# Batch 1 of a Fourier mixing kernel put into the quarter-matrix form of the batches after it

## The chip, the cores and the metric

The kernel runs on one core of one Trainium2 chip. The metric is the device time of one execution in microseconds (us), as the median of several runs; less is better. TensorE (PE in the profile, its weight loads PEld) multiplies matrices, VectorE (DVE) and ScalarE (ACT) work on rows of 128 partitions, GpSimd (POOL) does the same for data in SBUF, and SyncE (SP) issues most DMAs.

## The reference

There are two stages, both in 32-bit floating point. The input x has 8 batches of 3008 rows with 256 channels.

```python
X = np.fft.fft(x, axis=1)
X = np.fft.fft(X, axis=2)
attn = X.real                      # (8, 3008, 256) -> (24064, 256)
h = attn @ w_in                    # (256, 2048)
g = np.where(h > 0, h, np.exp(np.minimum(h, 0)) - 1)
out = g @ w_out                    # (2048, 256)
```

## The kernel before

**The main loop.** The real part of a two-dimensional transform is even under a joint reversal of row and channel, so the kernel computes only half of the output rows' frequencies, 1504 for each batch, and gets the mirrored rows from the same products. These 8 x 1504 = 12032 columns pass in 47 tiles of 256 columns. A tile takes 8 steps, each for two blocks of 128 of the 2048 hidden columns; a step is called a slot here, 376 in all. In a slot TensorE runs P (`mm_P`, weights Wc against the ring Rr), Q (`mm_Q`, weights Ws against the ring Ir, added into the same PSUM bank H), and seven more products of 256 columns into four accumulators (eight products in the first 16 slots). Between P and Q, VectorE must read the bank: `even_part` computes E = Rb * wex + H, where Rb holds the extra channel (number 128) and wex the last row of the folded weights. TensorE's Q waits for that. Then VectorE forms the mirrored half (`h_minus`, called h in the schedule), ScalarE does the negative parts and exponentials (b+, b-, x+, x-), VectorE the two results (`g_plus` and `g_minus`, g+ and g-), and GpSimd four sums of 128x256 for the products.

**The transform.** The rings Rr, Ir and Rb hold 2048 columns of transformed rows, and are filled ahead of the main loop. For each batch there are four transforms: cosine or sine (`ri`), and even or odd frequencies (`kodd`). Batches 2 to 7 are done in the *quarter* form: rows are loaded in eight classes (`load_quarter`, `load_odd`, near and far halves; `quarter_row`, a ScalarE copy, mends one row), mirrored rows are added (`mirror_sum`, GpSimd), the two halves are added or subtracted (`half_sum`, VectorE), channels are folded (`channel_fold`, GpSimd; `channel_edge`, ScalarE), pairs of rows are combined or twisted (`quarter_pairs`, `shift_pairs`), and then class `Quarter` multiplies by the matrices QM: two halves of four matmuls each, 94 to 188 columns wide. Its results are unfolded by VectorE and written into the rings (`plus`, `minus`). Batches 0 and 1 are done in the older form: class `Dft` multiplies by the matrices MC, two halves of three matmuls each, up to 378 columns wide. For batch 1 the rows come through `load_x` into the four tiles xl, `mirror_folds` makes the folds (tiles eo) with 30 GpSimd operations, and `at_half` places the halves.

**The extra channel.** `load_ext` gathers one channel of all batches as single elements, `fold_ext` and `dft_ext` transform it into one H bank, `ext_side` copies the bank's four parts into SBUF (parts 0 and 1 at slot 30, parts 2 and 3 at slot 33), and `ext_unfold`, `ext_up`, `ext_down`, `ext_rows` finish it on VectorE. It goes to DRAM, and `spread_ext` brings it into Rb and the last partition of Ir.

**The weights.** They are converted and folded in eight chunks in the first 16 slots. Row 127 of a folded chunk is needed as columns (wex). For chunks 0 and 1 two matmuls with a one-column operand do it (`turn_last_row`, then a ScalarE copy, `put_last_row`); for chunks 2 to 7 two DMAs through DRAM do (`spread_last_row`).

**What sets the order.** Nearly every call is an event `at(t, fn)`; events are sorted by t, and the order within each engine's queue is the order of issue. T = 4.8 is one slot. The beginning is a list of names by time (FRONT), where b-4 is b- of slot 4 and Wc3 the copy of chunk 3 into Wc; the main loop's operations have fixed offsets in a slot; row work of batches 2 to 7 is placed by slot numbers. The time t is no clock: an engine runs its queue in order and waits where data or a buffer is missing. H banks rotate through three buffers.

Of the kernel before, what the change touches and what calls it, by code (L numbers as in the profile page):

```python
# [9 lines left out]
FP = mybir.dt.float32  # L10
# [8 lines left out]
ND = 256  # L19
# [6 lines left out]
NE = 377  # L26
# [149 lines left out]
def kernel(  # L176
# [381 lines left out]
    def load_quarter_mats(ri, kodd):  # L558
        t = cpool.tile([128, BW], FP, tag=f"MC{ri}{kodd}", name=f"QM{ri}{kodd}")
        QM[ri, kodd] = t  # L560
        n = sum(QW[i % 2] for i in range(2 * ri + kodd))
        nc.sync.dma_start(
            out=t[0:96, 0 : QW[kodd]], in_=QM_dr.ap()[:, n : n + QW[kodd]]
        )
# [166 lines left out]
    def mirror_folds(L):  # L731

        ops = []
        rows = [t.rearrange("p (m d) -> p m d", d=ND) for t in L]
        for j, k in ((3, 2), (0, 1)):
            own, other = rows[j], rows[k][:, ::-1]
            for m in range(6):
                ops.append(
                    lambda own=own, other=other, m=m: gtt(
                        own[:, m, 1:], own[:, m, 1:], other[:, m, :0:-1], ALU.add  # L740
                    )
                )
            ops.append(
                lambda own=own, other=other: gtt(
                    own[:, :, 0:1], own[:, :, 0:1], other[:, :, 0:1], ALU.add
                )
            )
        EO = [None] * 4
        for kodd in range(2):
            z = L[1 + kodd]  # L750
            for n in range(4):
                c = slice(384 * n, 384 * n + 384)
                ops.append(
                    lambda z=z, c=c, kodd=kodd: gtt(
                        z[:, c], L[0][:, c], L[3][:, c],
                        ALU.subtract if kodd else ALU.add,
                    )
                )
            for ri in range(2):
                t = EO[2 * ri + kodd] = spool.tile(  # L760
                    [128, 768], FP, tag=f"{'eo'[ri]}{1 + 2 * kodd}", bufs=1, name="eo"
                )
                for h in range(2):

                    def fold(z=rows[1 + kodd], t=t, ri=ri, h=h):
                        src = z[:, 3 * h : 3 * h + 3]
                        lo, hi = (
                            v.rearrange("p m (d o) -> p m o d", o=2)
                            for v in (src[:, :, 1:129], src[:, :, 255:127:-1])
                        )  # L770
                        o = t[:, 384 * h : 384 * h + 384]
                        o = o.rearrange("p (m o d) -> p m o d", o=2, d=64)
                        if ri:
                            gtt(o, lo, hi, ALU.subtract)
                        else:
                            gtt(o, lo[:, :, ::-1], hi[:, :, ::-1], ALU.add)

                    ops.append(fold)
                if not ri:
                    o = t.rearrange("p (m o d) -> p m o d", o=2, d=64)  # L780
                    state["edge", kodd] = lambda o=o, z=rows[1 + kodd]: act(
                        o[:, :, 0, 63:64], z[:, :, 0:1]
                    )
        return EO, ops

# [12 lines left out]
    def half_sum(kodd, far, h):  # L798

        n = 94 if far else 96  # L800
        a, b, o = (lines(j, far)[0:n] for j in (0, 3, 1 + kodd))
        for m in (2 * h, 2 * h + 1):
            vtt(o[:, 3 - m], a[:, m], b[:, m], ALU.subtract if kodd else ALU.add)
# [34 lines left out]
    def quarter_pairs(b, ri, kodd, m):  # L838
# [4 lines left out]
        if not kodd:  # L843
            if m == 1:
                state["pairs"] = spool.tile(
                    [128, 384], FP, tag="side", bufs=2, name="pairs"
                )
            new = state["pairs"]
            a, z = (
                t[0:94, 128:512].rearrange("p (m d) -> p m d", d=128)  # L850
                for t in (near, far)
            )
            o = new[0:94].rearrange("p (m d) -> p m d", d=128)
            if m == 1:
                gtt(o, a, z[:, ::-1], ALU.add)
            else:
                gtt(z[:, ::-1], a, z[:, ::-1], ALU.subtract)
            for k in (1, 2, 3):
                parts["u", k] = new[0:94, 128 * k - 128 : 128 * k]
                parts["v", k] = slot(8 - k)  # L860
            return
# [371 lines left out]
    def ext_side(g, rows=NB):  # L1233
        kodd, par = EXT[g]
        n = NO if kodd else NE if par else 2 * NH
        t = spool.tile([128, 384], FP, tag="side", bufs=2, name="side")
        act(t[0:rows, 0:n], state["ext"][32 * g : 32 * g + rows, 0:n])
        state["side", par] = t

    def ext_unfold(kodd, tt, rows=NB):  # L1240
        n = NO if kodd else NE
        h = (n + 1) // 2
        even = state["side", 0]
# [4 lines left out]
    def ext_rows(kodd, tt, rows=NB):  # L1248
        n = NO if kodd else NE
        if not kodd or rows < NB:  # L1250
            rx = spool.tile([128, HALF + 1], FP, tag="rx", bufs=1, name="rx")
            state["rx"] = rx[0:rows]
        rx, a, b = state["rx"], state["es"], state["side", 1][0:rows]
        o, base = 1 - kodd, kodd * RUN
        m = n - 2 * o
        tt(rx[:, base : base + n], a[:, 0:n], b[:, 0:n], ALU.add)
        top = base + RUN - 1
        tt(rx[:, top : top - m : -1], a[:, o : o + m], b[:, o : o + m], ALU.subtract)
        if not kodd:
            tt(rx[:, HALF:], a[:, 0:1], b[:, 0:1], ALU.subtract)  # L1260
            nc.sync.dma_start(
                out=r4_dr.rearrange("o b -> b o"), in_=rx[:, HALF : HALF + 1]
            )
        nc.sync.dma_start(
            out=r128_dr[0:rows, base : base + RUN], in_=rx[:, base : base + RUN]
        )

    def ext_up():
        rx = state["rx"] = spool.tile(
            [128, HALF + 1], FP, tag="rx", bufs=1, name="rx"  # L1270
        )[0:NB]
        a, b = state["es"], state["side", 1][0:NB]
        vtt(rx[:, 0:NE], a, b[:, 0:NE], ALU.add)
        vtt(rx[:, HALF:], a[:, 0:1], b[:, 0:1], ALU.subtract)

    def ext_down():
        rx, a, b = state["rx"], state["es"], state["side", 1][0:NB]
        vtt(
            rx[:, RUN - 1 : RUN - 1 - (NE - 2) : -1],
            a[:, 1 : NE - 1], b[:, 1 : NE - 1], ALU.subtract,  # L1280
        )
        nc.sync.dma_start(
            out=r4_dr.rearrange("o b -> b o"), in_=rx[:, HALF : HALF + 1]
        )
        nc.sync.dma_start(out=r128_dr[0:NB, 0:RUN], in_=rx[:, 0:RUN])
# [398 lines left out]
    def open_x(b):  # L1684
        state["L"], state["loads"] = load_x(b)

# [47 lines left out]
    names["L"] = lambda: [open_x(1)] + [state["loads"][n]() for n in (4, 5)]  # L1734
    for n in range(4):
        names[f"L{n}"] = lambda n=n: state["loads"][n]()
    for slot in range(8):
# [37 lines left out]
        (16.44, "w3p u3b Wc2 Xb1 b+3 w3R h3"),  # L1775
        (17.88, "w4b b-3 J-even u1M w4l w3s x-3"),
        (19.2, "P4 x+3 u2l u2b w3M Xa2 u3d V4"),
        (20.51, "w4d g-3 u2d w3P Q4 g+3 J-copy"),
        (21.72, "w4a Xb2 b+4 u2R J-sum w4p h4"),
        (23.12, "x+4 f3 u2a L1 P5 g+4 Ws3"),  # L1780
# [3 lines left out]
        (28.7, "b-5 P6 w4s u3p L2 J-odd x-5"),  # L1784
        (30.87, "V6 w4M Xa4 g+5"),
        (32.25, "u3s L3 Q6 w4P g-5 Xb4 b+6 h6 J-up J-down u3M"),
# [34 lines left out]
    for c, t in ((2, 15.2435), (3, 23.1265)) + tuple((c, (2 * c - 1) * T + 0.04) for c in range(4, 8)):  # L1821
        at(t, lambda c=c: spread_last_row(c))
    for i in range(8):
        at((12.9 + 0.5 * i) * T + 3.6, lambda i=i: sum_weights(i))
# [73 lines left out]
    def at_half(step, d, par, col):  # L1898
        assert step + 1 >= safe(col)
        t = step * T  # L1900

        def run():
            d().ps = bank("H")
            d().mms(par, d().ps)

        at(t + 4.75, run)
        if par:
            at(t + T + 1.01, lambda: d().plus())
            at(t + T + 1.02, lambda: d().minus())
        else:  # L1910
            at(t + T + 0.9, lambda: d().copy())
            at(t + T + 1.0, lambda: d().unfold())

    def at_dft(step, gap, b, ri, kodd, stat):
        box = []

        def d():
            if not box:
                box.append(Dft(ri, b, kodd, stat()))
            return box[0]  # L1920

        at_half(step, d, 0, 0)
        at_half(step + gap, d, 1, b * HALF + (kodd + 1) * RUN)

    def begin_folds():
        L = state["L"]
        state["EO"], state["ops"] = mirror_folds(L)

# [5 lines left out]
    at(11 * T + 3.55, lambda: ext_rows(1, gtt, 1))  # L1934
    at(11 * T + 3.6, lambda: spread_ext(0, 1))
    for n in range(16):
        j, k = divmod(n, 4)
        at(
            (14.4 + 0.5 * n) * T,
# [7 lines left out]
    at(30 * T + 4.25, lambda: ext_unfold(0, vtt))  # L1947
    at(31 * T + 4.25, ext_up)
    at(32 * T + 4.25, ext_down)
# [159 lines left out]
```

## Time and profile before

| | us |
|---|---|
| median of 3 runs | 1909.23 (1909.05 to 1913.21) |
| the profiled execution | 1909.52 |
| its span, first to last instruction | 1907.7 |
| TensorE busy | 1899.9 (100%) |
| VectorE busy | 1466.4 (77%) |
| GpSimd busy | 1348.9 (71%) |
| ScalarE busy | 877.1 (46%) |

The granted TensorE clock is full throughout. In the profile a 32-bit matmul appears as two records. A line of a timeline gives the start in us from the span's beginning, the duration of the stretch, engine, line, operation, what is written from what, shapes, and the number of instructions merged; in brackets stands the idle time before it and what ended it. Line 592 is the helper that issues every matmul, 598, 601 and 604 are those for VectorE, GpSimd and ScalarE. Slot numbers against time in the trace: slot 6 begins at 60.2 us, slot 8 at 73.5, slot 10 at 86.8, slot 12 at 98.1, slot 14 at 110.3, slot 30 at 193.6, slot 33 at 207.95.

### The profile page before, as it was taken

Reading aid. Unit: us, or ns where it says so; the run is one execution under the profiler, and the core shown is the slowest. Engines: PE = TensorE matmul, PEld = TensorE weight load, DVE = VectorE, ACT = ScalarE, POOL = GpSimd, SP = SyncE. Lnnn points to the kernel's source line nnn. Section 1 sums busy time; section 2 is a strip of 40 time slices with the busy share of each in tenths; the row PEclk is TensorE's granted clock in tenths of the full one; section 3 lists DMA queues with packets and bytes.
Section 4 is the critical chain, followed back from the end, with each engine's and each line's share of the span. In section 5 each row is a group of like instructions: output and inputs, shape, how many; then the busy total and the mean of one; then the engine's idle time right before and its main releaser. Section 6 shows DMA issues by size and latency. Waiting matters only on the chain.

```text
span 1907.7 us, 27911 instructions
## 1 busy us (share of the span) xinstructions
PE 1899.9 (100%) x8972; PEld 1649.8 (86%) x8972; DVE 1466.4 (77%) x2788; ACT 877.1 (46%) x1711; POOL 1348.9 (71%) x1834
## 2 busy tenths in 40 slices
PE   9999999999999999999999999999999999999999
PEld 6888888888888888888888888888888888888887
DVE  8766667887878878778777787877878778777666
ACT  5754444444444444444444444444444444444443
POOL 4887667786677766777667777687766777556664
PEclk9999999999999999999999999999999999999999
DMA  8145211211011110111112111022110210100101
GB/s 339 45 33 43 57 24 45 52 24 36 12 44 41 32 33 12 46 40 30 31 19 49 34 28 30 13 56 44 24 24 16 55 20 16 17 12 15 20 12 23
DMA packets 278934, 73.80 MB, mean 39 GB/s; under 512 B 254402, under 2 KB 268998, under 8 KB 278788
## 3 DMA queue, kind: packets, MB, share of 16 engines
q1 hardware_dynamic: 270148, 61.58, 15.9%
q0 software_dynamic: 6464, 10.18, 1.7%
q8 instruction: 71, 1.16, 0.3%
q14 instruction: 75, 0.61, 0.1%
q10 hardware_dynamic: 2176, 0.26, 0.1%
HBM read 47.10 MB, written 24.80 MB: 38 GB/s over the span
## 4 chain that ended last, share of the span: by engine, by line
PE 97%; DVE 2%; DMA 0%; issue 0%; ACT 0%; POOL 0%; ACTq 0%; POOLq 0%; DVEq 0%
PE H L592 38%; PE pB L592 17%; PE pC L592 17%; PE pD L592 17%; PE pA L592 9%; DMA xl<-in_x_dram,ix 0%; DVE e L689 0%; DVE o L689 0%; POOL w L601 0%; DVE E L1339 0%; DVE pow L460 0%; DVE w L418 0%; DVE v L598 0%; DVE u L598 0%; ACT Wsc L604 0%
## 5 line engine op out<-in xcount | busy, mean ns | idle before, releaser
L601 POOL TENSOR_TENSOR G<-G 128x256 f32<-128x256 f32 x1437 | 1045.8, 737 | 504.1 <-DVE G L1369 346.9
L604 ACT ACTIVATE G<-H 128x512 f32<-128x512 f32 x376 | 224.4, 597 | 929.1 <-DVE G L1353 925.5
L1339 DVE SCALAR_TENSOR_TENSOR E<-Rb,wex,H 128x256 f32<-128x256 f32 x752 | 327.6, 477 | 334.3 <-PE H L592 327.6
L592 PE MATMUL H<-Rr,Wsc 128*128 128x256 f32 x1504 | 387.7, 380 | 0.5 <-ACT Wsc L604 0.5
L592 PE MATMUL H<-Ir,Wsc 128*128 128x256 f32 x1504 | 386.8, 380 | 1.0 <-DVE E L1339 1.0
L592 PE MATMUL pC<-G,WT 128*128 128x256 f32 x1440 | 369.6, 379 | 0.0
L592 PEld LDWEIGHTS H<-Ir,Wsc 128*128 128x128 f32 x1504 | 278.4, 189 | 48.9 <-DVE E L1339 3.4
L592 PEld LDWEIGHTS H<-Rr,Wsc 128*128 128x128 f32 x1504 | 282.1, 190 | 41.6 <-issue 2.3
L592 PEld LDWEIGHTS pC<-G,WT 128*128 128x128 f32 x1440 | 273.6, 190 | 37.2
L1353 DVE SCALAR_TENSOR_TENSOR G<-E,H 128x512 f32<-128x512 f32 x376 | 256.9, 683 | 45.1 <-POOL G L601 11.5
L1369 DVE SCALAR_TENSOR_TENSOR G<-G,H 128x512 f32<-128x512 f32 x376 | 255.8, 680 | 39.6 <-ACT G L604 39.5
L1369 DVE SCALAR_TENSOR_TENSOR G<-M,G 128x512 f32<-128x512 f32 x376 | 256.6, 682 | 0.7 <-ACT M L604 0.7
L604 ACT ACTIVATE G<-G 128x512 f32<-128x512 f32 x376 | 233.4, 621 | 0.0
L592 PE MATMUL pA<-G,w 128*128 128x256 f32 x784 | 229.4, 379 | 0.0
L592 PE MATMUL pB<-G,w 128*128 128x256 f32 x784 | 229.4, 379 | 0.0
L592 PE MATMUL pD<-G,w 128*128 128x256 f32 x784 | 229.3, 379 | 0.0
L604 ACT ACTIVATE M<-G 128x512 f32<-128x512 f32 x376 | 224.2, 596 | 2.8 <-DVE G L1353 1.5
L604 ACT ACTIVATE M<-M 128x512 f32<-128x512 f32 x376 | 221.1, 588 | 0.1
L592 PE MATMUL pB<-G,WT 128*128 128x256 f32 x720 | 214.4, 379 | 0.0
L592 PE MATMUL pD<-G,WT 128*128 128x256 f32 x720 | 214.2, 379 | 0.0
L592 PEld LDWEIGHTS pA<-G,w 128*128 128x128 f32 x784 | 148.9, 190 | 20.7 <-DVE G L1369 0.3
L592 PEld LDWEIGHTS pB<-G,w 128*128 128x128 f32 x784 | 148.9, 190 | 20.4 <-PE H L592 0.2
(172 smaller groups left out, 1555.3 us busy)
## 6 DMA issues: line engine op xcount, KB each, us to landing
out_dram<-ot SPq DMA_DIRECT2D x496, 32.0 KB
xq<-in_x_dram SPq DMA_DIRECT2D x48, 94.0 KB
out_dram<-ot SPq DMA_DIRECT2D x256, 2.0 KB
Rb<-r SPq DMA_DIRECT2D x10, 376.0 KB
raw<-in_moe_w_in_dram SPq DMA_DIRECT2D x7, 512.0 KB
MC<-dft_mats SPq DMA_DIRECT2D x3, 943.5 KB
xq<-in_x_dram SPq DMA_DIRECT2D x12, 192.0 KB
xq<-in_x_dram SPq DMA_DIRECT2D x36, 64.0 KB
```

The source lines that it names most:

```text
L592: nc.tensor.matmul(out_, lhsT=lhsT, rhs=rhs, start=start, stop=stop, skip_group_check=True)
L601: pin(nc.gpsimd.tensor_tensor(out=o, in0=a, in1=b, op=op))
L604: pin(nc.scalar.activation(out=o, in_=i, func=func, **kw))
L1339: nc.vector.scalar_tensor_tensor(out=S.E[:, c], in0=Rb[:, cols(i)], scalar=wex[:, f : f + 1], in1=S.H[:, c], op0=ALU.mult, op1=ALU.add,)
L1353: nc.vector.scalar_tensor_tensor(out=two(S.G[:, 0:512])[:, :, ::-1], in0=two(S.E), scalar=2.0, in1=two(S.H), op0=ALU.mult, op1=ALU.subtract,)
L1369: nc.vector.scalar_tensor_tensor(out=o, in0=e, scalar=-1.0, in1=h, op0=ALU.add, op1=ALU.max)
```

## The change

Batch 1 takes the quarter form. `mirror_folds`, `open_x`, `at_half`, `at_dft` and `begin_folds` go; batch 1's loads, sums, folds, pairs and twists become a table of single times, and four calls of `at_quarter` place its transforms. The four QM matrices are packed into the homes of MC[1,0] and MC[1,1] and loaded at slot 7.2 in place of slots 51 to 60; the twist table and the index tables of the quarter loads come early too. For batch 1 the combined pairs go into free columns of the fold tiles in place of a `side` buffer. The extra channel's bank is copied in one go at slot 30: parts 2 and 3 then go into the free part of the tile rx, and its later steps are cut into `ext_up`, `ext_down`, `ext_put` and placed by the table. Its element loads begin 0.8 slot later. For weight chunks 6 and 7 the last row is turned by TensorE.

```diff
-    def load_quarter_mats(ri, kodd):
...
+    def load_quarter_mats():
+        n = 0
+        home = [
+            cpool.tile([128, BW], FP, tag=f"MC1{i}", name=f"QM{i}") for i in range(2)
+        ]
+        for ri in range(2):
+            for kodd in range(2):
+                w = QW[kodd]
+                c = 0 if ri else QW[1 - kodd]
+                QM[ri, kodd] = t = home[ri == kodd][:, c : c + w]
+                nc.sync.dma_start(out=t[0:96], in_=QM_dr.ap()[:, n : n + w])
+                n += w
...
-    def mirror_folds(L):
...
     def ext_side(g, rows=NB):
         kodd, par = EXT[g]
         n = NO if kodd else NE if par else 2 * NH
-        t = spool.tile([128, 384], FP, tag="side", bufs=2, name="side")
+        if kodd and rows == NB:
+            t = state["rx"][:, RUN + NO * (1 - par) :]
+        else:
+            t = spool.tile([128, 384], FP, tag="side", bufs=2, name="side")
...
-    names["L"] = lambda: [open_x(1)] + [state["loads"][n]() for n in (4, 5)]
+    names["L"] = lambda: [
+        fn(1, j, 0) for j in (3, 0) for fn in (load_quarter, load_odd)
+    ]
...
-    for c, t in ((2, 15.2435), (3, 23.1265)) + tuple((c, (2 * c - 1) * T + 0.04) for c in range(4, 8)):
+    for c, t in ((2, 15.2435), (3, 23.1265)) + tuple((c, (2 * c - 1) * T + 0.04) for c in (4, 5)):
         at(t, lambda c=c: spread_last_row(c))
+    for c in (6, 7):
+        at((2 * c - 1) * T + 3.02, lambda c=c: turn_last_row(c))
+        at((2 * c - 1) * T + 3.03, lambda c=c: put_last_row(c))
...
-            (14.4 + 0.5 * n) * T,
+            (15.2 + 0.5 * n) * T,
             lambda j=j, k=k: load_ext(j, 192 * k, 192 * (k + 1)),
...
-    at(33 * T + 1.46, lambda: ext_side(2))
-    at(33 * T + 1.47, lambda: ext_side(3))
...
-    at(27 * T + 4.3, quarter_table)
-    at(34 * T, lambda: nc.sync.dma_start(out=twist_tab[0:96], in_=QT_dr.ap()))
...
-    for step, ri, kodd in ((26, 0, 0), (34, 1, 0), (37, 0, 1), (42, 1, 1)):
-        at_dft(step, 2, 1, ri, kodd, lambda k=2 * ri + kodd: state["EO"][k])
...
+    at(30 * T + 1.48, ext_open)
+    for g in (2, 3):
+        at(30 * T + 1.49, lambda g=g: ext_side(g))
+    at(10.0, quarter_table)
+    at(7.2 * T, load_quarter_mats)
+    at(8 * T, lambda: nc.sync.dma_start(out=twist_tab[0:96], in_=QT_dr.ap()))
...
+    for t, fn, *key in (
+        (22.73, mirror_sum, 3, 0, 3),
+        (25.32, quarter_row, 1),
...
+        (36.22, mirror_sum, 0, 0, 2),
+        (38.68, half_sum, 1, 0, 1, vtt),
+        (39.31, half_sum, 1, 0, 0, vtt),
+        (40.40, channel_fold, 0, 1, 0, 0),
+        (44.12, half_sum, 0, 0, 1, vtt),
...
+        (148.01, ext_unfold, 0, vtt),
+        (153.06, ext_up, 0, vtt),
+        (157.11, ext_down, 0, vtt),
...
+        (279.33, ext_put, 1),
+        (279.72, spread_ext, 1, 1),
+    ):
+        at(t, lambda fn=fn, key=key: fn(*key))
+
+    for step, ri, kodd, finish, join in ((28, 0, 0, 0, 31), (34, 1, 0, 0, 37), (38, 0, 1, 42, 53), (44, 1, 1, 50, 54)):
+        at_quarter(step, 1, ri, kodd, finish, join)
```

## The prediction

> **What bounds the kernel now.** I read the page's first part and its chain first.
>
> ```profile
> span 1907.7 us, 27911 instructions
> PE 1899.9 (100%) x8972; PEld 1649.8 (86%) x8972; DVE 1466.4 (77%) x2788; ACT 877.1 (46%) x1711; POOL 1348.9 (71%) x1834
> ...
> PE 97%; DVE 2%; DMA 0%; issue 0%; ACT 0%; POOL 0%; ACTq 0%; POOLq 0%; DVEq 0%
> ```
>
> TensorE is busy all the time and is 97% of the chain. The end moves only by matmul time removed or added, and by gaps in TensorE's stream. Busy time counts overlapping records, so I price a group of matmuls by its spacing: from its first start to the start of what follows. The timeline of TensorE has one half of a batch 1 transform (three matmuls, two records each), and one of batch 2:
>
> ```profile
> 173.20 1.44 PE L592 MATMUL H<-MC,eo 128*128 128x189 f32 x6
> 174.48 1.02 PE L592 MATMUL H<-Rr,Wsc 128*128 128x256 f32 x4
> ...
> 431.88 0.36 PE L592 MATMUL H<-QM,e 95*128 95x95 f32 x2
> 432.07 0.39 PE L592 MATMUL H<-QM,o 94*128 94x95 f32 x2
> 432.30 0.39 PE L592 MATMUL H<-QM,pairs 94*128 94x95 f32 x2
> 432.52 0.39 PE L592 MATMUL H<-QM,o 94*128 94x94 f32 x2
> 432.74 1.06 PE L592 MATMUL H<-Rr,Wsc 128*128 128x256 f32 x4
> ```
>
> 174.48 - 173.20 = 1.28 us against 432.74 - 431.88 = 0.86 us. Then the gaps: lines of TensorE's timeline with a wait in brackets, and of VectorE's.
>
> ```profile
> 60.21 1.13 PE L592 MATMUL H<-Rr,Wsc 128*128 128x256 f32 x4 [0.54 <-ACT Wsc L604]
> ...
> 101.58 1.13 PE L592 MATMUL H<-Ir,Wsc 128*128 128x256 f32 x4 [0.69 <-DVE E L1339]
> ...
> 215.49 1.13 PE L592 MATMUL H<-Ir,Wsc 128*128 128x256 f32 x4 [0.31 <-DVE E L1339]
> ```
>
> ```profile
> 99.45 0.43 DVE L406 TENSOR_SCALAR pow<-raw 128x512 int32<-128x512 int32 x1 [2.15 <-POOL w L601]
> ...
> 112.11 0.87 DVE L1339 SCALAR_TENSOR_TENSOR E<-Rb,wex,H 128x256 f32<-128x256 f32 x2 [1.43 <-DMA wex<-wx]
> ```
>
> A 256-column matmul starts every 0.432 us. What the spacing shows beyond that, the restart included, is 0.8 us before 60.2 (slot 6), 0.96 us before 101.6 (slot 12), 0.23 us at 112.7 (slot 14) and 0.7 us before 215.5 (slot 34). From 216 to 1497 no gap passes 0.1 us, although five batches with quarter matrices lie there. These four, 2.7 us, are all that scheduling can win in the stretch that the change touches.
>
> **What the Trainium skill says.** (1) TensorE: Matmul & The Clock Gate, section LDWEIGHTS: a load takes columns/1.2 ns, 107 for 128 columns, whatever the rows. The trace agrees on rows (192 ns for 94x128, 190 for 128x128; these records overlap). Eight records at 107 ns would be 0.86 us, an estimate that matches the spacing: narrow quarter matmuls are bound by weight loads, so fewer columns save less than in proportion. (2) SBUF — State Buffer, section SBUF: two separate sides: a VectorE operation with two SBUF inputs and a GpSimd operation that reads SBUF exclude each other for a whole instruction. The trace agrees: the same VectorE adds of 256 columns take 482 to 949 ns. (3) DMA: Bandwidth & Descriptors, section Anatomy of one DMA: about 2.0 us fixed, given for GpSimd's path. Here SyncE's wex copy, issued at 109.96, releases VectorE at 112.11: 2.15 us.
>
> **Part 1, matmuls of batch 1.** Out go 24 with MC, in eight groups of 1.28, 1.90, 1.28, 1.91, 1.26, 1.90, 1.27 and 1.90: 12.70 us. In come 32 with QM, as in every later batch: 0.86, 1.09, 0.87, 1.08, 0.87, 0.87, 0.87, 0.86: 7.37 us. All of it lies on the path: **-5.33 us**, the surest term.
>
> **Part 2, last weight row of chunks 6 and 7.** Two DMAs each go (wx, then wex); two 128x1 matmuls and a ScalarE copy (0.17 us, hidden, ScalarE is 46% busy) each come. The same pair starts at 35.24 and the next matmul at 35.71, 0.47 us: **+0.94** for both. The wait at 112.11 goes: **-0.23**. The H bank of folds[6] and folds[7] is kept half a slot longer and is wanted two slots later: 0.
>
> **Part 3, extra channel.** Before, sides 2 and 3 (0.98 us of ScalarE at 209.84) and the p copy stood ahead of an exponential at 210.73; VectorE idled 1.48 us for it, E came late, TensorE lost 0.7 us. They move to slot 30; slot 33 has the p copy alone, as later tiles, which don't stall there: **-0.7** (0 if the twists put there refill it). At slot 30 four copies of 0.47 us end near 195.7: g+ starts 0.65 us late, and the VectorE work up to the E of 199.5 still fits: 0 (at worst +0.5). The bank freed earlier makes room for the quarter transforms. The put of the second half moves to slot 58.2; slot 64 needs it: 0.
>
> **Part 4, row work of batch 1.** *GpSimd*: out 22 xl operations (12 at 0.94, 8 at 1.00, 2 at 0.30 us) and 8 eo at 1.18, 29 us; in 16 mirror sums at 0.72, 4 edges at 0.2, 16 folds at 0.84 and the pairs, about 4.6 together: 30 us. The total stays. *VectorE*: 16 half-sum adds, 20 twists and the quarter's unfolds come, long unfolds and puts go; by mean spacings +5 us in slots 7 to 10, +5 in 20 to 28, +14 in 28 to 46, +4 to 58. In slots 28 to 46 that is 81 us of work in about 99, 82%; between 431 and 520, where batch 2 does the same, VectorE was busy 69.30 of 89.00 us and TensorE had no gap. The cover is VectorE's wait for H before each E; where it is gone, a late E costs TensorE its lateness. I take **+0.4** (0 to 2). *SyncE and DMA*: 4 row loads and the 4 copies of part 2 go, 32 row loads come; net 24 at about 0.4 us, 10 us of SyncE's queue, mostly before slot 15, while the DMA engines are 2 to 52% busy. The element loads of the extra channel queue behind them, and are set 0.8 slot later. GpSimd reads their result at 187.4 and TensorE at 191.6, cover 3.2 us after GpSimd's 1 us: 0. Four QM loads (0.36 us each) move from 214 to 277 back to before slot 16; they wait for the last use of MC[1,0] and MC[1,1], near 63 us, and batch 1 wants them at slot 29: 0. Twist table and iotas (0.5 us of SyncE and GpSimd, idle early): 0.
>
> **Part 5, the front.** Slot 6: ScalarE's row copy (0.39 us, spacing 0.30) now stands between b-4 and x-4 in the chain x-4, g-4, h5, b+5, Wc3 that TensorE awaits: **+0.3** (0 to 0.4). Slot 8: two half-sum adds stand ahead of E, which followed at 74.85 without any idle and may start at 75.2 at the latest (Q at 76.09 less 0.87). Two adds at 0.41 us free or 0.72 contended (the operation before them was, 1.51 us) make it 0.45 to 1.1 late, with restart up to 1.2, and slot 9's E is then near its limit: **+1.1** (0 to 2). The next four adds fall into the 2.89 us that VectorE idled before 87.98: 0. Slot 12: E stood behind a VectorE step that waited for GpSimd's multiply at 98.14, which waited for ScalarE (96.69); less GpSimd work doesn't shorten this. But the first pair of part 2 lies between slots 11 and 12 and uses up half of that gap: **-0.47** (-0.96 to 0).
>
> **Sum**: -5.33 + 0.94 - 0.23 - 0.7 + 0.4 + 0.3 + 1.1 - 0.47 = -4.0 us. The profiled execution took 1909.52 us (1907.7 between first and last instruction), 0.3 above the median 1909.23; applied to the median this gives **1905.2 us**. With every open term at its better end: -5.33 + 0.94 - 0.23 - 0.7 - 0.96 = -6.3, 1902.9; all at the worse: -5.33 + 0.94 - 0.23 + 0.5 + 2 + 0.4 + 2 = +0.3, 1909.5. A measurement of this kernel tells some 0.3%, 5.7 us, from no change, so the likeliest gain lies inside that.
>
> **Rivals.** *A, the gaps close* (0.33): slot 8 has room, slots 12, 14 and 34 close: 1902.9 to 1903.5. For it: three of four gaps lose a cause. Against: VectorE had no idle before slot 8. *B, the gaps only move* (within the forecast): -4.4 plus as much new gap as old goes, 1904.8, up to 1909. *C, slower* (0.10): VectorE becomes the bound in slots 33 to 46, where each E stands behind twists and puts. If each is as late as at 215.5, 0.7 us, 14 slots cost 9.8, and -4.0 + 9.8 = +5.8: 1915. From 0.7 us of mean lateness in all 14 it decides. Against: the same work leaves no gap in batches 2 to 7. *D, it does not do what it says*: the order of the built instructions has 24 MC matmuls fewer, 32 QM and 4 one-column matmuls more, so 0.
>
> **How the numbers follow.** Forecast with B 0.57 (within 0.3%), A 0.33 (faster), C with milder relatives 0.10 (slower). The range 1902.8 to 1908.3 takes the better end and most of the worse; all bad terms together, and C, stay out.
>
> **What would show it.** Right: no MC,eo rows; QM groups of 0.86 to 1.09 us between slots 28 and 48; 0.47 us for a pick pair; no wait for wex near 112 and no gap near 215; VectorE about 28 us busier, GpSimd equal; a new gap at slot 8. Wrong: a row of waits for E in slots 31 to 50, or TensorE waiting for the extra channel.

## The result, and the profile after

The change makes the kernel slower: 1921.88 us median of six runs (1919.13 to 1923.29) against 1909.17 for the kernel before (six runs, 1909.05 to 1913.21). The ratio is 1.0063, 95% interval 1.0053 to 1.0073. The forecast was 1905.2 with a range up to 1908.3, so the sign is wrong. The profiled execution took 1920.93 us.

First the page's first and fourth part, of the changed kernel:

```profile
span 1919.1 us, 28089 instructions
PE 1899.6 (99%) x8996; PEld 1651.3 (86%) x8996; DVE 1497.3 (78%) x2854; ACT 878.7 (46%) x1717; POOL 1355.9 (71%) x1846
PE 91%; DVE 2%; DMA 2%; SPq 2%; issue 1%; POOL 1%; ACT 0%; ACTq 0%; DVEq 0%; POOLq 0%
```

TensorE's busy time is the same within 0.3 us, and its share of the chain fell from 97% to 91%: the lost time is waiting, and DMA and SyncE's queue (SPq) are now in the chain. TensorE's waits, in total, times, longest:

```profile
PE H L598 <- DVE E L1285: 6.3, 4, 2.3
PE H L598 <- POOL xe L607: 6.3, 1, 6.3
PE H L598 <- ACT Wsc L610: 1.3, 2, 0.7
```

These five waits for E and xe are in TensorE's timeline (start, stretch, line, idle time before it and its end in brackets), beside two rows that the prediction asked for, a pair of `turn_last_row` and a half of a batch 1 transform:

```profile
52.71 1.13 PE L598 MATMUL H<-Ir,Wsc 128*128 128x256 f32 x4 [2.26 <-DVE E L1285]
...
81.94 1.13 PE L598 MATMUL H<-Ir,Wsc 128*128 128x256 f32 x4 [1.93 <-DVE E L1285]
...
97.24 1.13 PE L598 MATMUL H<-Ir,Wsc 128*128 128x256 f32 x4 [1.62 <-DVE E L1285]
...
104.25 0.50 PE L598 MATMUL H<-pick,Wsc 128*128 128x1 f32 x4
...
109.68 1.13 PE L598 MATMUL H<-Ir,Wsc 128*128 128x256 f32 x4 [0.50 <-DVE E L1285]
...
191.81 0.36 PE L598 MATMUL H<-QM,e 95*128 95x95 f32 x2
...
192.68 1.06 PE L598 MATMUL H<-Rr,Wsc 128*128 128x256 f32 x4
...
203.88 3.92 PE L598 MATMUL H<-MC,xe 128*8 128x189 f32 x24 [6.26 <-POOL xe L607]
207.73 1.13 PE L598 MATMUL H<-Rr,Wsc 128*128 128x256 f32 x4
```

What released VectorE's E in slots 4 and 10, and what it did before slot 8's E; and what GpSimd waited for at slot 30:

```profile
51.78 0.87 DVE L1285 SCALAR_TENSOR_TENSOR E<-Rb,wex,H 128x256 f32<-128x256 f32 x2 [2.27 <-DMA wex<-wx]
...
77.18 2.19 DVE L418 TENSOR_SCALAR w<-raw 128x512 int32<-128x512 int32 x1
79.29 1.81 DVE L604 TENSOR_TENSOR xq<-xq,xq 96x256 f32<-96x256 f32 x2
81.03 0.86 DVE L1285 SCALAR_TENSOR_TENSOR E<-Rb,wex,H 128x256 f32<-128x256 f32 x2
...
96.32 0.87 DVE L1285 SCALAR_TENSOR_TENSOR E<-Rb,wex,H 128x256 f32<-128x256 f32 x2 [2.47 <-DMA wex<-wx]
...
107.54 0.43 DVE L406 TENSOR_SCALAR pow<-raw 128x512 int32<-128x512 int32 x1 [2.08 <-POOL w L607]
```

```profile
203.08 0.39 POOL L607 TENSOR_TENSOR xs<-xs 128x96 f32<-128x96 f32 x1 [9.19 <-DMA xq<-in_x_dram]
```

That line names a row load (xq) as the releaser. It can't be: the operation reads xs. The releaser is inferred from semaphores, and SyncE's queue shows which DMA it was, the last copy into xs, issued at 200.56. Here is that queue before (first fence) and after (second), cut to the extra channel's loads and what stands ahead of them. L1169 and L1126 are the element loads, L1197 and L1154 the copies into xs:

```profile
110.39 6.37 SPq L1169 DMA_DIRECT2D x<-in_x_dram  x4
...
180.42 0.58 SPq L1197 DMA_DIRECT2D xs<-xe_dr  x1
```

```profile
114.41 0.24 SPq L1231 DMA_DIRECT2D r<-rx  x1
119.00 0.65 SPq L334 DMA_DIRECT2D xq<-in_x_dram  x1
119.69 0.96 SPq L317 DMA_DIRECT2D xq<-in_x_dram  x2
...
127.17 0.63 SPq L334 DMA_DIRECT2D xq<-in_x_dram  x1
127.84 3.16 SPq L317 DMA_DIRECT2D xq<-in_x_dram  x7
131.47 6.33 SPq L1126 DMA_DIRECT2D x<-in_x_dram  x4
...
200.56 0.58 SPq L1154 DMA_DIRECT2D xs<-xe_dr  x1
```

The chain of element loads starts 21.1 us later and ends 20.1 us later. It takes the same 70 us in both kernels: 71 DMAs before and 74 after go through SyncE's queue between its first and last issue, 40 of them output stores. Last, the clock, from the windows view of the changed kernel (length; busy us of PE, PEld, DVE, ACT, POOL; granted clock; DMA share; GB/s):

```profile
50.00:53.80 3.80, 1.54 (x8) 1.03 (x7) 2.02 (x5) 1.31 (x4) 3.72 (x5) 1.00 0.13 46
53.80:57.00 3.20, 3.20 (x10) 2.49 (x9) 3.20 (x7) 1.84 (x3) 1.50 (x2) 0.50 0.96 251
...
203.60:207.70 4.10, 3.82 (x24) 1.52 (x24) 0.00 (x0) 0.00 (x0) 3.29 (x6) 0.54 0.20 52
```

After the wait of slot 4, and in the extra channel's matmuls, TensorE runs at half clock (0.50 in the column behind the engines) for over 3 us. A wait of 2.3 us costs 4 us.

**Where the time went.** The starts of slots (first matmul of P) give a table by stretch that doesn't depend on when the first weights arrive. From run to run that arrival moves the start of slot 0 (the first slot) between 26.2 and 28.5 us, so single runs are compared below by these stretches and not by their totals. All runs of this study, one trace each, in us (x130 to b_xlate were executed once, the last four 6 or 21 times):

| kernel | slots 3-5 | 5-9 | 9-11 | 11-15 | 15-29 | 29-61 | 0-61 |
|---|---|---|---|---|---|---|---|
| before | 12.49 | 25.21 | 13.41 | 22.78 | 71.01 | 164.41 | 324.32 |
| after | 16.71 | 27.55 | 15.30 | 23.24 | 68.64 | 169.82 | 336.25 |
| x130 | 16.69 | 27.56 | 15.17 | 23.35 | 68.64 | 176.38 | 342.78 |
| x144 | 16.68 | 27.55 | 15.05 | 23.48 | 68.63 | 173.08 | 339.46 |
| pinrows | 17.03 | 27.55 | 13.41 | 23.68 | 68.63 | 173.11 | 338.43 |
| hs8 | 18.37 | 26.49 | 16.75 | 23.68 | 68.64 | 170.74 | 339.65 |
| late2 | 16.75 | 27.53 | 14.46 | 24.06 | 68.64 | 163.51 | 329.93 |
| x118d | 17.13 | 27.55 | 14.69 | 23.86 | 92.71 | 161.64 | 352.57 |
| pick25 | 13.45 | 29.61 | 13.86 | 23.34 | 68.64 | 168.53 | 332.43 |
| b_xlate | 12.49 | 25.22 | 13.41 | 22.77 | 71.03 | 174.27 | 334.20 |
| latepick | 13.45 | 27.97 | 13.86 | 23.34 | 68.63 | 162.78 | 325.04 |
| best | 13.46 | 26.18 | 15.69 | 24.89 | 68.64 | 162.78 | 326.63 |
| best2 | 13.45 | 26.23 | 15.51 | 24.19 | 68.63 | 163.00 | 326.00 |
| dmapin | 14.00 | 32.44 | 13.41 | 23.81 | 68.64 | 162.97 | 330.26 |

(Slots 0 to 2 take 15.0 in all of them; each column runs from the start of its first slot to the start of its last.) The change costs +4.22 at slot 4, +2.34 mostly at slot 8, +1.89 at slot 10, +0.46 in slots 11 to 15 and +3.04 from slot 15 to 61, in all +11.93. From slot 61 on the two traces differ by less than 0.1 us.

### The profile page after: what moved, and what is told of

It is laid out like the page before. It is cut to its first block, busy times and chain, and to the rows that moved or that the text cites. A ratio compares the mean times of both kernels' runs of the same rounds, so it can differ in the third digit from the quotient of the medians.

```text
span 1919.1 us, 28089 instructions
## 1 busy us (share of the span) xinstructions
PE 1899.6 (99%) x8996; PEld 1651.3 (86%) x8996; DVE 1497.3 (78%) x2854; ACT 878.7 (46%) x1717; POOL 1355.9 (71%) x1846
## 4 chain that ended last, share of the span: by engine, by line
PE 91%; DVE 2%; DMA 2%; SPq 2%; issue 1%; POOL 1%; ACT 0%; ACTq 0%; DVEq 0%; POOLq 0%
PE H L598 35%; PE pB L598 16%; PE pC L598 16%; PE pD L598 16%; PE pA L598 8%; SPq L1520 1%; DMA x<-in_x_dram 1%; SPq L1126 0%; DMA xl<-in_x_dram,ix 0%; DVE E L1285 0%; POOL w L607 0%; DMA wex<-wx 0%; DMA xq<-in_x_dram,ix 0%; DVE e L695 0%; DMA xq<-in_x_dram 0%
```

## The experiments

**Does the extra channel's chain stand behind the row loads?** Two runs moved its element loads forward.

```diff
-            (15.2 + 0.5 * n) * T,
+            (13.0 + 0.5 * n) * T,        # x130;  (14.4 + 0.5 * n) * T in x144
```

x130: 

> One size changed: the extra channel's sixteen element loads are set from slot 13.0 on instead of 15.2, which puts the first of them ahead of the second set of far row loads in SyncE's queue. Theory T1 (head of line: the element loads stand behind row loads that wait until 127.2 us for their tile): the first element load leaves near 118 to 121 us instead of 131.5, the last copy into xs near 188 instead of 200.1, the 6.3 us wait of TensorE for xe before slot 30 goes with the half clock behind it, -8.3 us: about 1912.6. Theory T3 (the added row loads take the DMA engines' throughput): the element loads take correspondingly longer, the wait stays, 1920 to 1921.

x144: 

> One size changed back: the element loads of the extra channel are set from slot 14.4 on, as in the kernel before, instead of 15.2. Theory T2 (the shift by 0.8 slot, about 5 us, makes the chain late): the last copy into xs moves from 200.1 to about 195, and of the 6.3 us wait of TensorE some 1.3 us stay: about 1914 to 1916. Theory T1 (head of line): only one of the four first element loads gets ahead of the far row loads, the other three stay behind them and their wait until 127.2 us, so the wait stays at 5 us or more: 1919.5 to 1921.

Measured: both got worse. TensorE's wait for xe grew to 12.44 us (x130) and 9.45 us (x144), and slots 29 to 61 took 6.6 and 3.3 us more than in the changed kernel. The single times were 1928.71 and 1926.06. The first element load left at 128.8 and 130.3, or 3.5 and 4.3 us after the start of slot 15 (7.4 in the changed kernel): it was still behind the row load that leaves near 128. The other element loads did not come out earlier, because six far row loads now stood among them: 80 DMAs instead of 74 between first and last issue, 79.6 and 76.0 us instead of 69.7. So undoing the shift by 0.8 slot doesn't remove the wait, and a place further forward in the order doesn't by itself bring the end forward. My T1 expected -8.3 and was wrong in that form; no theory had expected either run to get slower.

**Move the producers ahead of nearly everything, or move the consumer.** In late2 the fold, the matmuls, the copies and the three VectorE steps stand two slots later; in x118d all sixteen element loads stand ahead of most far row loads.

```diff
-    at(29 * T + 1.35, fold_ext)
+    at(31 * T + 1.35, fold_ext)      # late2; dft_ext, ext_side, ext_open likewise
...
-        (148.01, ext_unfold, 0, vtt),
+        (157.61, ext_unfold, 0, vtt),
```

```diff
-            (15.2 + 0.5 * n) * T,
+            (11.78 + 0.25 * n) * T,      # x118d
```

late2: 

> Consumer moved, producers left: the fold of the extra channel on GpSimd, its matmuls, the four bank copies and the three VectorE steps behind them stand two slots (about 10.4 us) later; the element loads stay where they are. Theory T1, in the form that the first four runs leave (SyncE's queue hands out some 74 DMAs in about 70 us from the first element load on, whatever stands first; the load chain is late because it starts 21 us later, at 131.5 instead of 110.4): the last copy into xs is still issued near 200, lands near 203, GpSimd is done by 204.1 and TensorE asks for it near 207: no wait for xe, no half clock, -8.3 us in the stretch from slot 28 to 34. Rival (the wait belongs to the place, such as GpSimd's or ScalarE's order in slot 30): a wait of several us for xe or for E shows up again in slots 31 to 33.

x118d: 

> Producers moved: all sixteen element loads are set from slot 11.78 on, a quarter of a slot apart, right behind the store of the first channel row, so that they stand ahead of most far row loads and of all output stores. T1 (start of the chain decides): first element load near 121.5 (the row of the ring and one far row load are still ahead of it), last copy into xs issued 70 us later, near 191 to 193, wait of TensorE at slot 30 under 1 us, -7 to -8 us. Rival T3 (throughput of the DMA engines: 6144 four-byte elements for each quarter of the channel keep them busy): the far row loads behind the elements land late, GpSimd's and VectorE's mirror sums of slots 18 to 24 wait for them, and the wait at slot 30 shrinks by less than half.

Measured, late2: the matmuls with xe follow without a wait and at full clock.

```profile
209.98 2.09 PE L598 MATMUL H<-MC,xe 128*8 128x189 f32 x24
...
219.67 0.70 PE L598 MATMUL pB<-G,WT 128*128 128x256 f32 x2 [0.92 <-POOL G L607]
```

Slots 29 to 61 take 6.3 us less than in the changed kernel. The 8.2 us (from where xe was wanted, 197.55, to 207.73, less the 2.02 us that these matmuls take at full clock) are gone; 2 us come back as two waits for GpSimd's sums, of which the second line shows the first. The loads themselves were not touched, so lateness against a fixed consumer is all there is to this wait.

Measured, x118d: 1937.72, 16 us worse than the changed kernel. The first element load left at 123.0 and TensorE didn't wait for xe, but the row loads behind the elements landed late, as T3 had it. GpSimd's timeline of x118d, and TensorE's:

```profile
146.98 0.89 POOL L607 TENSOR_TENSOR xq<-xq,xq 94x255 f32<-94x255 f32 x2 [4.71 <-DMA x<-in_x_dram]
...
168.99 0.72 POOL L607 TENSOR_TENSOR xq<-xq,xq 94x255 f32<-94x255 f32 x1 [18.97 <-DMA xq<-in_x_dram]
```

```profile
150.07 1.22 PE L598 MATMUL pB<-G,WT 128*128 128x256 f32 x2 [3.00 <-POOL G L607]
170.44 1.22 PE L598 MATMUL pD<-G,w 128*128 128x256 f32 x2 [14.88 <-POOL G L607]
```

GpSimd's mirror sums wait for rows, its sums G stand behind them in the same queue, and TensorE waits for those. Issuing slowed as well: an element load took 1.61 us of SyncE's queue on average (1.06 in the changed kernel), a row load 1.82 (0.86). Whether the queue or the DMA engines behind it set that pace isn't separated. In every order tried here either the rows or the elements came late between slots 12 and 30.

**Is the late start enough without the new rows?** One size changed in the kernel before:

```diff
-            (14.4 + 0.5 * n) * T,
+            (16.9 + 0.5 * n) * T,        # b_xlate
```

> The kernel before, with one size changed: the element loads of the extra channel are set from slot 16.9 on instead of 14.4; no other part of the change is in it. The changed kernel's first element load left 12.8 us later against the slots than before (7.4 us after slot 14's start instead of 5.3 us ahead of it). If the late start alone is sufficient for the wait at slot 30: before, the last copy into xs was issued at 180.4 and, with some 2.5 us to landing and 1.2 us on GpSimd, was about 7 us ahead of TensorE's 191.3; a start about 13 us later makes TensorE wait 5 to 7 us there and, with the half clock behind it, about +7 to +9 us: 1916 to 1918. Rival (the added row loads are needed for it, as they lengthen the chain or use the DMA engines): the chain is shorter than 70 us when the loads stand closer together, and the wait stays under 2 us, 1909 to 1911.

(What this text calls slot 14's start is the start of slot 15 in the count used elsewhere.) Measured: 1919.13 us, 10 us slower than the kernel before. The first element load kept its place at 109.8, the second left at 133.5; the last copy into xs was issued at 196.1.

```profile
199.46 3.48 PE L592 MATMUL H<-MC,xe 128*8 128x189 f32 x24 [8.39 <-POOL xe L601]
```

The wait of 8.39 us is a little over the 5 to 7 that were expected. A late start of this chain is sufficient, without a row of batch 1 in the quarter form. From the second load on it still took 63 us.

**Why does wex land late in slots 4 and 10?** In pinrows the single-row loads of batch 1 keep the program's order, so those of slot 9 leave behind chunk 5's wex copy; in pick25 the last rows of chunks 2 and 5 go by TensorE.

```diff
-                nc.sync.dma_start(                 # load_odd
+                pin(nc.sync.dma_start(             # pinrows, for b == 1
```

```diff
-    for c, t in ((2, 15.2435), (3, 23.1265)) + tuple((c, (2 * c - 1) * T + 0.04) for c in (4, 5)):
+    for c, t in ((3, 23.1265), (4, 7 * T + 0.04)):      # pick25
...
-    for c in (6, 7):
+    at(17.95, lambda: turn_last_row(2))
+    at(17.96, lambda: put_last_row(2))
+    for c in (5, 6, 7):
```

pinrows: 

> One thing changed: the single-row loads of batch 1 are held to the order of the program, so that those of slot 9 go out behind chunk 5's wex copy and not between wx and wex; at chunk 2 (slot 4) the row loads stay between the two, which makes slot 4 the control. Theory W1 (the row loads ahead of wex in the queue or in the DMA engines delay its landing): wex of chunk 5 is issued at about 89.5 us, lands within 3.5 us, and the 1.9 us gap of slot 10 goes, -1.9 us: 1919.0; the gap of slot 4 stays with its half clock. Rival W2 (wex lands late for another reason, such as a wait for a queue that the trace does not show, or the GpSimd gathers): wex lands 5 us or more after its issue as before and the gap of slot 10 stays above 1 us: 1920 to 1921. What the delayed row loads then do to SyncE's queue behind them is open, +-1 us.

pick25: 

> One part widened: the last weight row of chunks 2 and 5 is turned by TensorE (two one-column matmuls and a ScalarE copy each), as chunks 6 and 7 are, and no longer by two DMAs; row loads unchanged. If the 2.4 us gap at slot 4 (with its half clock, 4.0 us in all) and the 1.9 us gap at slot 10 come from the late landing of wex, both go and 0.94 us is added for two pairs: -5.0 us. Rival (E of slot 4 or 10 is held by VectorE or by H as well): over 1 us of either gap stays.

SyncE's queue in slot 9, in the changed kernel and then in pinrows:

```profile
88.56 0.22 SPq L647 DMA_DIRECT2D wx<-Wsc  x1
88.90 1.27 SPq L334 DMA_DIRECT2D xq<-in_x_dram  x2
90.71 0.39 SPq L650 DMA_DIRECT2D wex<-wx  x1
```

```profile
89.25 0.22 SPq L652 DMA_DIRECT2D wx<-Wsc  x1
90.35 0.38 SPq L655 DMA_DIRECT2D wex<-wx  x1
```

With the two 94-row loads between, wex was issued at 90.71 and released VectorE at 96.32, 5.6 us later. Without them slot 10's E (94.62 in pinrows) follows VectorE's work without idling, and slots 9 to 11 take 13.41 us, exactly as before the change. Slot 4, the control, kept its gap. W1 holds for slot 10. Of the 2.47 us that VectorE had idled there, 1.05 lay in the wait for a turn (2.15 us from the issue of wx to that of wex, against 1.10 in pinrows); the rest lay in the landing. The total did not gain (1923.59): the element chain ended later (203.1 against 201.1), TensorE wanted its result 0.8 us earlier and waited 9.05 us for it. In pick25 both gaps went as well: slots 3 to 5 fell by 3.26 and slots 9 to 11 by 1.44. What is left over the kernel before is 0.45 in slots 9 to 11, one pair, and 0.96 in slots 3 to 5, a pair and a new TensorE wait of 0.35 us behind it for ScalarE's copy. The single time is 1919.08, and the table has -3.8 where -5.0 was expected; part of the difference is that after the unchanged 1.93 us wait of slot 8 the clock now fell to half. The view below cuts the time into windows of 3.41 us, first of the changed kernel and then of pick25 ("Missing: the clock" below says why at these places):

```profile
77.69:81.11 3.42, 2.32 (x11) 1.71 (x9) 3.42 (x4) 2.61 (x5) 3.34 (x5) 1.00 0.00 0
81.11:84.52 3.41, 2.58 (x12) 2.30 (x13) 3.41 (x7) 0.00 (x0) 2.15 (x2) 1.00 0.00 0
84.52:87.93 3.41, 3.41 (x18) 3.00 (x17) 3.41 (x8) 2.63 (x5) 1.28 (x1) 1.00 0.02 5
```

```profile
79.12:82.53 3.41, 1.48 (x8) 1.10 (x7) 3.41 (x7) 0.54 (x2) 2.65 (x4) 1.00 0.00 0
82.53:85.94 3.41, 3.41 (x10) 2.69 (x9) 3.41 (x6) 1.28 (x3) 2.11 (x2) 0.50 0.02 5
```

**Slot 8.** Three runs moved the half-sum adds that stand ahead of slot 8's E: hs8 moved one pair behind that E, best one pair there and one behind slot 9's E (with the parts of latepick), best2 put all four on GpSimd and also moved two of the extra channel's copies on ScalarE behind two exponentials.

```diff
-        (38.68, half_sum, 1, 0, 1, vtt),
+        (39.45, half_sum, 1, 0, 1, vtt),     # hs8
```

hs8: 

> One step moved: the first pair of half-sum adds of batch 1 on VectorE is set behind slot 8's E instead of ahead of it. If the two adds ahead of E make the gap of 2.2 us at slot 8, E starts at about 79.3 and the gap goes: -2.2 us, 1918.7. Rival: VectorE is short of time in slot 8 or 9 whatever stands first (mantissa steps of 2.19 us under contention), then the gap moves behind E or into slot 9: 1920 to 1921.

latepick: 

> Two of the tried parts together in the changed kernel: the extra channel's fold and matmuls two slots later, and the last row of chunks 2 and 5 by TensorE as well. By the spacings of the single runs (-6.3 us and -3.8 us, the latter with 1.6 us of half clock after slot 8 in it) about 10 us less than the changed kernel: 1911 to 1913, if the two do not touch. Rival: with the slots earlier by 5 us against SyncE's queue, the element chain is late again at slot 32, and 2 to 4 us come back: 1914 to 1916.

best: 

> As latepick, and the first two pairs of half-sum adds of batch 1 on VectorE taken away from ahead of slot 8's E: one pair stands behind that E, the other behind slot 9's, so that slot 8 and slot 9 have two and six adds. If the 2.1 us gap of slot 8 comes from the pair ahead of E and slot 9 has room for six (VectorE idled 1.6 us before its E and 0.6 us before slot 10's): -2 us and no half clock there (-1.6): 1907.5 to 1909.5, level with the kernel before or slightly faster. Rival (as the first run with the pair moved showed: the gap moves to slots 8 and 9 in full): 1911 to 1913.

best2: 

> As latepick, with two more edits. The four half-sum adds of slot 8 stand on GpSimd again, behind its mantissa multiply of that slot, where GpSimd idled 4.4 us (it waited for ScalarE); and the two copies of the extra channel's second half on ScalarE stand behind the next two exponentials of slot 32 instead of ahead of them. If the pair of adds ahead of slot 8's E made its 2.1 us gap, that gap goes without a new one, since VectorE loses 3 us of work; if the four copies ahead of an exponential make the 1.1 us wait for GpSimd at slot 33, that goes too: -2.1 and -0.8 us against latepick, 1908 to 1909, 1 us faster than the kernel before or level with it. Rival (VectorE and GpSimd are both full between slots 8 and 12, so work moved on either comes back as lateness): 1 to 2 us of new gaps in slots 9 to 12, 1910 to 1911.

Measured. hs8: slot 8's gap shrank to 0.36 us and two new ones, 0.66 and 1.26, came in slot 9; slots 3 to 15 took 2.5 us more than in the changed kernel, 1.7 of it at slot 4, ahead of the step that was moved and so not explained by it; the other 0.8 is 1.06 less in slots 5 to 9 and 1.9 more behind them. best: slots 5 to 9 fell by 1.8 against latepick, slots 9 to 15 rose by 3.4. (In best one fold reads rows of one class before they are summed; its time stands for the placing alone.) best2: -1.7 and +2.5, and its copies gained nothing (slots 29 to 61 took 0.2 more). The rival's account held each time, the work comes back as lateness, though hs8 as a whole was slower than the rival's range. The four adds that follow slot 9's E show why, first in hs8, where GpSimd is idle at that point, then in best2, where it has the moved adds:

```profile
90.06 1.42 DVE L604 TENSOR_TENSOR xq<-xq,xq 96x256 f32<-96x256 f32 x4
```

```profile
82.86 4.26 DVE L604 TENSOR_TENSOR xq<-xq,xq 96x256 f32<-96x256 f32 x4
```

latepick came out as expected: 1911.04 us median of 21 runs against 1909.13 for the kernel before, ratio 1.0007 (1.0000 to 1.0013), the lowest of those tried. best was 1.0012 (1.0005 to 1.0018), best2 1.0011 (1.0005 to 1.0018), so the three can't be told apart. None beats the kernel before.

**Closing slots 4 and 10 by order alone.** dmapin has late2's edits, the last rows of chunks 2 to 6 by DMA, and all row and QM loads of batch 1 in program order, one row class of them moved behind chunk 2's wex.

> The other way to close the gaps of slots 4 and 10: the last rows of chunks 2 to 6 go by DMA (only chunk 7 by TensorE), and all row loads and QM loads of batch 1 are held to the order of the program, with the loads of one row class moved behind chunk 2's wex copy, so that no row load stands between a wx and its wex or ahead of it by less than 2 us; the extra channel's fold and matmuls two slots later, as in late2. If row loads ahead of wex were the whole cause of both gaps: slots 3 to 5 take 12.5 us as in the kernel before (16.7 in the changed one), slots 9 to 11 take 13.4 (15.3), no TensorE pair is paid for chunks 2, 5 and 6 (0.47 us each), slot 8's 2.1 us stay: from slot 1 to slot 61 about 323 us against 324.3 in the kernel before, 1908 to 1909. Rival (wex is late for its own reason, or the row loads are now late for GpSimd's sums): gaps of over 1 us at slots 4, 10 or 12 to 16, 1911 or more.

(Its "slot 1 to slot 61" is the table's last column.)

Measured: 1915.96 us, ratio 1.0035 (1.0022 to 1.0047); the rival held. VectorE didn't wait for wex in slots 4 and 10, and slots 9 to 11 took 13.41 us. But the moved row class now came late: its two gathers stand ahead of a weight multiply on GpSimd, and GpSimd waited 3.04 us for its rows at 58.58, with the next weight multiplies behind that. TensorE waited for weights instead, in slots 4 and 6 (the second with half clock behind it), and after the wait of 1.94 us in slot 8 the clock fell to half as well:

```profile
51.38 1.99 PE L605 MATMUL pA<-G,w 128*128 128x256 f32 x8 [1.24 <-POOL w L614]
...
64.18 1.49 PE L605 MATMUL H<-Rr,Wsc 128*128 128x256 f32 x4 [2.18 <-ACT Wsc L617]
```

## Why the prediction was wrong

**The step that failed is Part 4, "SyncE and DMA", in its last sentences**: the added issues were put at 10 us of SyncE's queue, the element loads "queue behind them", and then the cost was 0 because of a "cover 3.2 us". Both terms were wrong, and they can be worked out now, against the start of slot 15 (115.73 before, 124.04 after). *The cover*: the last copy into xs had been issued by 181.0; about 2 us to landing and 0.9 on GpSimd make xe ready near 183.9, against the first matmul with xe at 191.58, so 7.7 us. I had read 3.2 from when GpSimd came to it in its own order. *The delay*: the end of issue moved from 65.3 to 77.1 us after that start, 11.8, and TensorE asks 2.3 us earlier (73.5 instead of 75.8), since batch 1's narrower matmuls shorten the stretch. 11.8 + 2.3 - 7.7 = 6.4 us, against 6.26 us in the timeline; with the restart and half clock in the matmuls behind it, 8.2. I counted the new row loads by issue time (0.4 us each). What counts in an in-order queue is how long each waits there: 4.3 us ahead of the load at 119.0 and 5.6 us ahead of that at 127.2, in which a row load waited for GpSimd's gather into the same tile, with everything behind it held. GpSimd issues these two gathers between its own operations, at 109.61 and 117.16. The trace before has no wait for a gather in SyncE's queue. But it shows that the same row loads of the later batches wait long in this queue, here for VectorE (in total, times, longest):

```profile
SPq L334 <- DVE xq L598: 89.2, 6, 17.3
```

An unknown wait needed a bound on its bad side; it got 0 and nothing else. Of the 15.9 us between the forecast's -4.0 and the table's +11.9, this step is 8.2.

**Missing from the sum: wex of chunks 2 and 5** (+4.22 and +1.89). Part 2 priced the chunks whose way changed and no others. Row loads between wx and wex stretched the landing of wex from 2.15 us, the value of the trace before, to 5.6. The Trainium skill's DMA: Bandwidth & Descriptors, section Anatomy of one DMA, gives about 2.0 us fixed; the 2.15 agrees with that, and the 5.6 behind two row loads doesn't, so the figure is no price for a copy with row loads just ahead of it.

**Missing: the clock.** For slot 8 a gap was priced at its length plus 0.1 us of restart. The spacing shows 0.26 of restart (2.2 us for the wait of 1.93), and behind some waits half clock. When it comes can be worked out. In all fourteen traces the times at which the clock changes lie whole multiples of 3.413 us apart: in the changed kernel at 53.80, 57.21, 200.57 and 207.40, that is 1, 42 and 2 steps. So the clock changes only at the edges of a grid of windows, and the grid lies differently against the kernel from run to run. With each trace cut along its grid, half clock followed on every one of the 19 full-clock windows in which TensorE idled for 1.93 us or more, and on none with 1.77 us or less. That settles why equal waits end differently. In the changed kernel an edge at 81.11 cuts the wait of slot 8 into 1.1 and 0.8 us; in pick25 the same 1.93 us lie within one window, 79.12 to 82.53. (In dmapin, too, the 1.94 us lie within one; in latepick an edge cuts them.) The price is 1.7 us, half of a window. latepick's 21 executions show it without a trace: eight with a mean clock of 1.000 took 1908.8 to 1909.8 us, thirteen with 0.999 took 1910.5 to 1912.7, and the medians differ by 1.7. The Trainium skill's TensorE: Matmul & The Clock Gate, section What's actually happening, says that the activity window is free-running and 3413 ns long; the traces agree. Its section HAM oscillation warns of idle gaps above about 3.4 us; here 1.93 us within a window were enough, and the measurement decides.

**Part 5, slot 8: mechanism right, size wrong.** +1.1 (0 to 2) was forecast, 2.2 measured. Two adds took 1.81 us where 1.44 was the worst case, and the mantissa step ahead of them 2.19 where it had taken 1.51: both beside GpSimd. This fits the exclusion that the Trainium skill's SBUF — State Buffer, section SBUF: two separate sides, describes, and the same four adds at 1.42 and 4.26 us show it better than the trace before did. Slot 6: +0.3 forecast, 0.14 measured. Slot 12: -0.47 forecast, -0.20 measured; VectorE's wait for GpSimd stayed (2.08 us at 107.54, 2.15 before), as argued.

**Right.** *Part 1*: the half at 191.81 takes 0.87 us; the stretch from slot 15 to 61 is +3.04, against 8.2 - 5.33 - 0.7 + 0.36 + 0.4 = 2.9 with the three small gaps of the next lines, so the -5.33 is all there. *Part 2*: a pair at 104.25 to 104.62 and the first matmul behind it delayed by 0.08, 0.45 us, and no wait for wex in slot 14. *Part 3*: the gap of slot 34 is gone, -0.7. *Part 4, VectorE*: two new gaps came, 0.36 at slot 32 (behind E) and 0.4 at slot 38 (for GpSimd's sums), 0.76 where +0.4 (0 to 2) was forecast. VectorE is 30.9 us busier (28 forecast), GpSimd 7.0 (0 forecast), and in slots 31 to 50 no other wait for E came, so rival C, which carried the chance of "slower", was false. "TensorE waiting for the extra channel" stood among what would prove the prediction wrong, but it had no price and no chance.

Sum: -5.33 + 0.94 - 0.23 - 0.7 + 0.36 + 0.4 + 0.14 + 2.2 - 0.2 + 4.22 + 1.89 + 8.2 = 11.9, against 11.93 in the table. The 4.22 and the 8.2 hold 1.7 us of half clock each.

**What stays open.** Which of the waits ahead of 131.5 matters most wasn't separated: taking the row loads' dependence on the gather away, or a second queue for them, wasn't tried. Where between 1.77 and 1.93 us of idle time in a window the clock begins to fall, no run shows. Nor is it shown why the gap of slot 4, with the row loads left as they were, varied between 2.2 and 3.9 us.

## What to carry to other kernels

A DMA that is added to an in-order queue is not paid by its issue time but by its own wait, and by the slack of whatever stands behind it: list for every queue the transfers with a fixed consumer, and take slack from when the data landed, not from when an engine came to read it. When such a chain is late, moving its producer forward may only push other transfers back; moving the consumer by two slots took the wait away at once. Compare single runs by stretches of the trace, and price a TensorE wait of about 2 us or more with up to 1.7 us on top, since the clock may fall behind it. For a wait near 2 us that depends on where the windows lie in that run, so one execution of such a kernel tells little.

## What the runs showed of the hardware

Loads of single four-byte elements are dear for the queue that issues them. The sixteen loads of 1536 elements (6 KB; one is split in two) took 1.13 us of SyncE's queue each on average in the kernel before, an output store 0.5, and the copies behind the loads waited 11 us for landings. From the first element load to the last copy into xs the queue took 69 to 73 us wherever the order was left as it is, and 76 to 87 us in the four runs that moved the loads. The first four alone took 6.33 us to issue in the changed kernel and 11.43 in x118d; what made the difference isn't shown.

VectorE's two-input adds of 256 columns took 0.36 us each with GpSimd idle and 1.07 us with GpSimd at the same kind of work, a factor of three. In best2 each of the four ended 0.28 us after a GpSimd operation did (83.66, 84.53, 85.40 and 86.84 us), as it would if the two took turns.

TensorE's granted clock changes only at the edges of windows of 3.413 us, and 1.93 us of idle time within one window were enough to halve it in the next.
